# Agent attention with a soft mixture of experts: 32-column tensor products, an earlier normalisation, column maxima read from PSUM, and a new order of all steps

## The chip, the cores and the metric

One core of one Trainium2 chip runs the whole kernel; nothing is shared with other cores. The metric is the device time of one execution in microseconds (us): first to last instruction plus what the launch adds. One execution is also recorded by the hardware profiler, and the views below are of that one.

## The reference

Four batches of 11456 tokens with 128 channels go through attention by way of 49 agents, and the result `x` goes through a soft mixture of 8 experts with 4 slots each.

```python
def sm(a, b):                              # softmax of scaled scores
    s = scale * (a @ b.transpose(0, 2, 1))
    e = np.exp(s - s.max(-1, keepdims=True))
    return e / (e.sum(-1, keepdims=True) + 1e-09)
agent_v = sm(agents, k) @ v                # (4, 49, 128)
x = sm(q, agents) @ agent_v                # reshaped to (45824, 128)
logits = x @ phi                           # 32 slots
d = softmax of logits over the tokens (columns)
c = softmax of logits over the slots (rows)
slot_out[e] = relu((d.T @ x)[e] @ w1[e]) @ w2[e]
return c @ slot_out                        # (45824, 128)
```

All data are 32-bit floats.

## The kernel before

The tokens of a batch lie in four streams and are cut into six groups, five of 16 cells and one of 10; a cell is 128 tokens. There are 24 such groups of keys and values (the k side) and 24 of queries (the q side). The work is written as small steps with two-letter names; the table `ORDER` (1280 steps before) is one fixed sequence of them, and each engine executes its share of that sequence strictly in order. Buffers with numbered slots (`BUFS`) are handed out along the same sequence. All large loads go through the queue of SyncE (SP), also in that sequence.

**The k side of a group.** `kx` and `kv` load the tiles `kt` and `vt` (1 MB each). `ks` makes scores `sk` on TensorE (PE) in 32-column tiles, four of which lie side by side in the array. `km` takes their maximum on VectorE (DVE, `kmx`); `kt`, `kr`, `kb`, `kn` bring the running maximum of each agent through a transpose (`mt`), a row (`row`) and a broadcast (`mc`). `ke` is the exponential on ScalarE (ACT, `es`), `kT` its transpose on DVE (`et`; for group 0 on PE and ACT, steps `kP`), `kE` the product with the values (`ev`), `kA` the accumulation. After a batch `kg` and `kh` make agent_v and its product with phi, kept as `bd_m`.

**The q side.** `qx` loads `qt`, `qs` makes scores `sq`, `qt` transposes them on DVE into `pt`, `qm` takes the maximum over the agents. The exponential is done either on ACT cell by cell with its sum (`qE`, the groups in `DEN_ACT`) or by GpSimd (POOL) and ACT over the whole tile (`qu`, `qe`), with the sum on DVE (`qw`). `qp` transposes `pt` on PE into `tp`, `qc` copies it out, `ql` multiplies by `bd_m` into `lq`. For the 19 groups in `SWAP` `qn` transposes `lq` on DVE into `lt`, in two halves, and `qg` multiplies `lt` by the reciprocal sums `rt` on POOL; the last five groups use another form of `ql` and `qn` (tile `lp`). `lt` then holds the logits. `qM` takes the maximum of every slot (`cm`), `cr` that of every token; `cu` and `ce` write exp(logit − row maximum) into `x_all`.

**Rounds.** One or two q groups make a round, 13 in all. `r1` merges the column maxima, `r2`, `r3` reduce them over the tokens, `rx`, `r4`, `r5` broadcast them back, `ru` and `re` make the column weights `dt`, `rm` multiplies them by `rt`, and `rg` adds their product with `pt` to `gp`.

**The end.** After the last round the rounds are put on one scale, the experts run (`w1`, `w2`, steps m…), and 24 chunks of output leave: sums and reciprocals `cd`, scaling on POOL, transposes `ct`, the product `po`, copies `ot`, and a store.

Of the kernel before, what the change touches and what calls it, by code (L numbers as in the profile page):

```python
# [16 lines left out]
S = E * SE  # L17
# [17 lines left out]
CO_AB = CO_ID + P  # L35
# [121 lines left out]
def tile_agent_attn_soft_moe(ctx, tc, qT, kT, vL, agT, phi, w1, w2, cst, out):  # L157
# [7 lines left out]
    nc.scalar.dma_start(out=ag, in_=agT)  # L165
    nc.scalar.dma_start(out=cs, in_=cst)
# [9 lines left out]
    sel_r = [cs[0:2, CO_R + 3 * i:CO_R + 3 * i + 3] for i in range(2)]  # L176
# [5 lines left out]
    m_all = keep.tile([S, NR + 1], F32, name="m_all")  # L182
    av = keep.tile([A, B, C], F32, name="av")
    bd_m = [keep.tile([P, 2, S + 1], F32, name=f"bd_m{i}") for i in range(2)]
    si = keep.tile([P, E, 32], F32, name="si")
    v_.memset(si, 0.0)
    for t in bd_m:
        v_.tensor_copy(out=t[:, :, S], in_=mask_ab)
# [17 lines left out]
    def op(fam, i, eng, cost, fn, deps=(), takes=(), gives=()):  # L206

        k = (fam,) + tuple(i)
        ops[k] = {"eng": eng, "cost": cost, "deps": list(dict.fromkeys(deps)), "takes": takes,
                  "gives": gives, "reads": {}}  # L210
        for tag, first in gives:
            ops[first]["reads"][tag] = ops[first]["reads"].get(tag, 0) + 1
        fns[k] = fn
        return k
# [20 lines left out]
    den_act = [i for i in DEN_ACT if i in SWAP]  # L235
# [3 lines left out]
    def k_ops(i):  # L239
# [25 lines left out]
        def kt():  # L265
            k["mt"] = tile_("m", [2, P], f"mt_{i}")
            t_.transpose(k["mt"], k["mx"], ident)

        def kr():
            k["row"] = sm.tile([2, 32], F32, name=f"row_{i}", tag="row")  # L270
            v_.tensor_reduce(out=k["row"], in_=k["mt"].rearrange("p (q a) -> p a q", q=4),
                             axis=AX.X, op=ALU.max)
            if g:
                v_.tensor_tensor(out=k["row"], in0=k["row"], in1=prev["row"], op=ALU.max)  # L274
# [28 lines left out]
        def kP(h):  # L303
            k["tp", h] = tile_("a", [P, 4, P], f"ktp_{i}_{h}")
            for j in range(4):
                t_.transpose(k["tp", h][:, j, :], k["e"][:, h, P * j:P * j + P], ident)
# [803 lines left out]
```

## Time and profile before

| | |
|---|---|
| runs | 332.74, 334.86, 336.35 us (median 334.86) |
| profiled execution, span | 332.0 us; the page gives no other time for it, so the median of the runs lies 2.9 us above its span |
| busy in the span | PE 274.5, DVE 264.7, ACT 195.7, POOL 139.8 us |
| moved | 104.18 MB, 314 GB/s over the span |
| granted TensorE clock | mean 0.934 |

Engines run beside each other, so busy times don't add up to the span; an engine that is busy in a stage for nearly all of it can set that stage's length. A group line of the profile names the source line, the engine, the operation, the tile written and the tiles read, then `xcount | busy us, mean ns of one | idle before it and what ended that idle time`. A 32-bit matmul of the source appears as two MATMUL instructions. PEld is the loading of weights, which lies beside PE. A matmul's form, such as 128\*32, gives the rows and columns of the array that it uses.

### The profile page before, as it was taken

The numbers are of one execution on the slowest core, as the hardware profiler recorded it, in microseconds if no ns is written. First come the engines' busy times: TensorE is split into PE (matmuls) and PEld (weight loads), VectorE is DVE, ScalarE is ACT, GpSimd is POOL, SyncE is SP. The second block draws the span as 40 slices with busy tenths as digits, with TensorE's granted clock in tenths as the row PEclk, the third lists the DMA queues.
The fourth block names the chain that finished last, engine by engine and source line by source line (L and its number), as shares of the span: only waits on it lengthen the run. The fifth ranks groups of instructions, "written<-read, shape, count | busy, mean of one in ns | idle before, by whom it ended". The sixth has DMA issues, their size and how long they took to land.

```text
span 332.0 us, 9455 instructions
## 1 busy us (share of the span) xinstructions
PE 274.5 (83%) x3821; PEld 152.7 (46%) x3821; DVE 264.7 (80%) x580; ACT 195.7 (59%) x613; POOL 139.8 (42%) x158
## 2 busy tenths in 40 slices
PE   1978978988998989898999989998978885866740
PEld 0234455544554455365556447467765551121210
DVE  0754675989998898999998988999949649998830
ACT  2496333484979685686956986374442246655540
POOL 0100001418382454638236938566886205343400
PEclk9999999999999999999999999999968999678555
DMA  7999899999979649989839990699400019999996
GB/s 298 423 409 359 319 395 418 421 410 402 393 275 397 216 135 423 411 340 358 360 121 424 360 400 5 218 408 424 176 0 2 2 77 415 423 414 422 410 424 265
DMA packets 15451, 104.18 MB, mean 314 GB/s; under 512 B 1840, under 2 KB 1968, under 8 KB 4016
## 3 DMA queue, kind: packets, MB, share of 16 engines
q1 hardware_dynamic: 14976, 102.95, 77.3%
q8 instruction: 30, 0.49, 0.6%
q10 hardware_dynamic: 432, 0.63, 0.5%
q14 instruction: 13, 0.11, 0.1%
HBM read 79.98 MB, written 23.59 MB: 312 GB/s over the span
## 4 chain that ended last, share of the span: by engine, by line
DVE 44%; PE 29%; DMA 11%; ACT 7%; POOL 4%; issue 3%; SPq 0%; ACTq 0%; DVEq 0%; POOLq 0%
PE ev L318 5%; DVE cm L536 5%; DMA out<-ot 5%; DVE pt L434 5%; PE sk L230 5%; PE sq L230 4%; ACT pt L460 3%; DVE mx L439 3%; DVE kmx L262 3%; DVE et L300 3%; DVE rm L541 3%; PE po L1025 3%; DMA qt<-qT 3%; DMA cs<-cst 3%; DVE row L274 3%
## 5 line engine op out<-in xcount | busy, mean ns | idle before, releaser
L460 ACT ACTIVATE pt<-pt,mx 128x49 f32<-128x49 f32 x160 | 51.4, 328 | 10.6 <-DVE mx L439 10.5
L230 PE MATMUL sq<-qt,ag 128*32 128x512 f32 (+1 forms) x384 | 48.1, 600 | 8.0 <-ACT ag L168 6.7
L1025 PE MATMUL po<-ct,sob 32*128 32x512 f32 (+1 forms) x192 | 35.4, 819 | 17.9 <-DVE ct L888 13.0
L230 PE MATMUL sk<-kt,ag 128*32 128x512 f32 (+1 forms) x384 | 46.9, 573 | 1.5 <-issue 0.9
L318 PE MATMUL ev<-vt,et 128*64 128x129 f32 x720 | 45.1, 276 | 3.3 <-DVE lt L490 1.4
L1030 ACT COPY ot<-po 128x1536 f32<-128x1536 f32 (+1 forms) x24 | 32.6, 1359 | 24.5 <-DVE ot L1029 24.5
L318 PEld LDWEIGHTS ev<-vt,et 128*64 128x64 f32 x720 | 39.3, 136 | 10.6 <-issue 2.3
L444 POOL TENSOR_TENSOR pt<-pt,mx 128x784 f32<-128x784 f32 (+1 forms) x14 | 19.3, 1378 | 57.6 <-DVE mx L439 55.6
L882 POOL TENSOR_TENSOR x_all<-x_all,cd 128x512 f32<-128x512 f32 (+1 forms) x24 | 23.9, 994 | 41.6 <-DVE cd L877 38.7
L262 DVE TENSOR_REDUCE kmx<-sk 128x1 f32<-128x512 f32 (+1 forms) x48 | 30.7, 641 | 9.2 <-PE sk L230 8.8
L544 POOL TENSOR_TENSOR x_all<-lt,rm 128x512 f32<-128x512 f32 (+1 forms) x24 | 24.2, 1015 | 25.3 <-DVE rm L541 21.4
L434 DVE STREAM_TRANSPOSE pt<-sq 128x512 f32<-128x512 f32 (+1 forms) x48 | 31.3, 660 | 4.1 <-PE sq L230 3.9
L511 ACT COPY pT<-tp 128x512 f32<-128x512 f32 (+1 forms) x48 | 25.4, 557 | 11.7 <-PE tp L504 11.5
L640 POOL TENSOR_TENSOR dt<-lt,mb 128x512 f32<-128x512 f32 (+1 forms) x24 | 28.7, 1212 | 7.4 <-ACT mb L634 7.1
L300 DVE STREAM_TRANSPOSE et<-es 128x512 f32<-128x512 f32 (+1 forms) x46 | 29.6, 650 | 1.9 <-ACT es L289 1.9
L460 ACT ACTIVATION_READ_ACCUMULATOR pt<-pt,mx 128x1 f32 x160 | 30.5, 191 | 0.0
L1025 PEld LDWEIGHTS po<-ct,sob 32*128 32x128 f32 x192 | 10.4, 240 | 42.5 <-ACT ot L1030 42.2
L289 ACT ACTIVATE es<-sk,nm 128x512 f32<-128x512 f32 (+1 forms) x48 | 29.3, 650 | 0.2
L495 POOL TENSOR_TENSOR lt<-lt,rt 128x512 f32<-128x512 f32 (+1 forms) x19 | 19.0, 999 | 23.0 <-DVE lt L490 22.9
L504 PE MATMUL tp<-cs,pt 128*128 128x128 f32 x180 | 27.2, 282 | 0.7 <-ACT pt L450 0.5
L504 PEld LDWEIGHTS tp<-cs,pt 128*128 128x128 f32 x180 | 19.3, 141 | 14.4 <-issue 4.2
L1029 DVE COPY ot<-po 128x512 f32<-128x512 f32 (+1 forms) x24 | 15.4, 643 | 12.6 <-DMA out<-ot 7.7
(123 smaller groups left out, 462.8 us busy)
## 6 DMA issues: line engine op xcount, KB each, us to landing
out<-ot SPq DMA_DIRECT2D x21, 1024.0 KB, 6.8
vt<-vL SPq DMA_DIRECT2D x20, 1032.0 KB, 10.0
qt<-qT SPq DMA_DIRECT2D x20, 1024.0 KB, 8.4
kt<-kT SPq DMA_DIRECT2D x20, 1024.0 KB, 7.0
w1s<-w SPq DMA_DIRECT2D x4, 1024.0 KB, 11.3
w2s<-w SPq DMA_DIRECT2D x4, 1024.0 KB, 12.0
vt<-vL SPq DMA_DIRECT2D x4, 645.0 KB, 8.4
kt<-kT SPq DMA_DIRECT2D x4, 640.0 KB, 7.5
```

The costliest lines, as they stand in the source:

```text
L230: t_.matmul(sp[32 * q4:32 * q4 + 32, :nt], ag[:, b, 32 * h:32 * h + 32], xv[:, q4, :], start=True, stop=True)
L262: v_.tensor_reduce(out=k["mx"][:, h:h + 1], in_=k["s"][h][:, :nt], axis=AX.X, op=ALU.max)
L289: s_.activation(out=k["e"][:, h, :nt], in_=k["s"][h][:, :nt], func=AF.Exp, bias=k["nm"][:, h:h + 1])
L300: v_.transpose(out=k["et"][:, :n, 32 * h:32 * h + 32], in_=k["e"][:, h, :nt].rearrange("p (t a) -> p t a", a=32))
L318: t_.matmul(k["ev"][o:o + 64, :], k["et"][:, c, :], k["v"][:, c, :], start=c < 2, stop=c >= n - 2)
L434: v_.transpose(out=q["pt"][:, :n, 32 * h:32 * h + 32], in_=q["s"][h][:, :nt].rearrange("p (t a) -> p t a", a=32))
L460: s_.activation(out=x, in_=x, func=AF.Exp, bias=q["mx"][:, c:c + 1], accum_out=q["dn"][:, c:c + 1])
L504: t_.transpose(q["tp", h][:, (c - h0) // 2, :], q["pt"][:, c:c + 2, :].rearrange("p c a -> p (c a)"), ident)
L511: s_.copy(out=q["pT"][:, h0 // 2:h1 // 2, :], in_=q["tp", h][:, :(h1 - h0) // 2, :])
L640: eng.tensor_tensor(out=q["dt"][:, :n], in0=q["lt"][:, :n, :], op=ALU.subtract, in1=r["mb"].unsqueeze(1).to_broadcast([P, n, S]))
L1025: t_.matmul(po[:, r, :32 * n], z["sob"][32 * r:32 * r + 32, :], z["ct", j][32 * r:32 * r + 32, :32 * n], start=True, stop=True)
L1030: s_.copy(out=ov[:, 1:4], in_=po[:, 1:4, :32 * n])
```

## The change

Four things are done at once, and with them the table `ORDER` (1248 steps now) is a new sequence throughout.

1. **32-column products.** `kE` is split into two 32-column matmuls per cell; the broadcasts `kb` and `r4` read zero-padded rows of 128 partitions in place of 2 or 32; the transpose path of group 0 (`KT_PE`) and the `lp` form of the last five groups are gone.
2. **Running row maximum.** The previous row goes through PE beside the new maxima, and one DVE reduction over five blocks replaces a reduction and a `tensor_tensor`.
3. **Normalised ahead of the transposes.** `qw` (ACT) and `qr` make the reciprocal, the new step `qN` multiplies `pt` on POOL, then `qp` follows. `qg` and `rm` are gone. `DEN_ACT` has 12 groups in place of 10.
4. **Column maxima from PSUM.** `qM` reduces `lq` as it lies in PSUM to one number per partition; `r1` and `rx` are gone, `r6` is new, and `qv` transposes both halves at once.

At the start the constants come in two pieces, `ag` goes through SP, and two copies into `bd_m` are gone.

```diff
-                o = 64 * (c % 2)
-                t_.matmul(k["ev"][o:o + 64, :], k["et"][:, c, :], k["v"][:, c, :], start=c < 2,
-                          stop=c >= n - 2)
+                for h in range(2):
+                    o = 64 * (c % 2) + 32 * h
+                    t_.matmul(k["ev"][o:o + 32, :], k["et"][:, c, 32 * h:32 * h + 32],
+                              k["v"][:, c, :], start=c < 2, stop=c >= n - 2)
...
+            if g:
+                t_.matmul(k["mt"][:, P:nq], ident[:, 0:2], prev["row"], start=True, stop=True)
+            t_.matmul(k["mt"][:, 0:P], k["mx"], ident, start=True, stop=True)
...
-            if g:
-                v_.tensor_tensor(out=k["row"], in0=k["row"], in1=prev["row"], op=ALU.max)
...
+        def qN():
+            x = q["pt"][:, :n, 0:A]
+            nc.gpsimd.tensor_tensor(out=x, in0=x, op=ALU.mult,
+                                    in1=q["rt"][:, :n].unsqueeze(2).to_broadcast([P, n, A]))
+            nc.gpsimd.memset(q["pt"][:, :n, A:A1], 1.0)
...
-            v_.tensor_reduce(out=q["cm"], in_=q["lt"][:, :n, :].rearrange("p c s -> p s c"),
-                             axis=AX.X, op=ALU.max)
+            v_.tensor_reduce(out=rs[ri]["cm"][:, g - gs[0]:g - gs[0] + 1], axis=AX.X, op=ALU.max,
+                             in_=q["lp"][:, :n // 2].rearrange("p j e t -> p (j e t)"))
...
+        e = o("qw", (), "A", qw, deps=(e,))
+        e = o("qr", (), "V", qr, deps=(e,))
+        e = o("qN", (), "G", qN, deps=(e,))
+        p0 = o("qp", (0,), "P", lambda: qp(0), deps=(e,), takes=("a",))
```

Two lines of the new table, from its start: `kx ks.0 ks.1 kx km.0 qx@1 km.1 qx kt kr ks.0 kb kn ke.0 qs.0@1 …`; the old one began `qx qx qs.0 qs.1 qx qt.0 qs.0 qt.1 qm kx …`.

On PE, in the second batch, these instructions stood in a row before (`ev` is the product with the values, `mt` and `mc` the running maximum, `tp` a transpose of `pt`, `t` the two steps of a round's maximum):

```order
L230 MATMUL sq_1_1140<-qt_1_1057,ag 32x512 x4
L267 MATMUL mt_1158<-cs,kmx_1105 2x128
L318 MATMUL ev_1160<-vt_1008,et_1091 64x129 x16
L279 MATMUL mc_1192<-cs,row_1178 32x3 x4
L504 MATMUL tp_0_1198<-cs,pt_1015 128x128 x4
L504 MATMUL tp_1_1206<-cs,pt_1015 128x128 x4
L619 MATMUL t_1_1217<-cs,cmr_0_1145 32x128
L230 MATMUL sk_0_1219<-kt_5_1154,ag 32x320 x4
L230 MATMUL sk_1_1227<-kt_5_1154,ag 32x320 x4
L481 MATMUL lq_0_1240<-pT_1138,bd_m_69 32x4x32 x8
L630 MATMUL t_1_1255<-cs,mrep_1250 128x32
```

About the same place of the program reads so now:

```order
L225 MATMUL sk_1_1303<-kt_5_967,ag 32x320 x4
L475 MATMUL lq_1308<-pT_1288,bd_m_75 32x4x32 x8
L475 MATMUL lq_1308<-pT_1288,bd_m_75 32x32 x8
L275 MATMUL mc_1336<-cs,row_70 32x3 x4
L304 MATMUL ev_1353<-vt_1209,et_1161 32x129 x32
L264 MATMUL mt_1386<-row_70,cs 2x32
L265 MATMUL mt_1386<-cs,kmx_1330 2x128
L225 MATMUL sq_0_1392<-qt_2_1176,ag 32x512 x4
L275 MATMUL mc_1399<-cs,row_71 32x3 x4
L225 MATMUL sk_0_1412<-kt_0_1254,ag 32x512 x4
L547 MATMUL t_2_1421<-cs,cm_1251 1x128 x2
```

Before, the output width goes 32, 2, 64, 32, 128, 32, 128; now the whole stretch has outputs of at most 32 columns, and `ev` counts 32 matmuls in place of 16.

On DVE, in the third batch before (`lt` are logits, `cm` and `cmr` column maxima of a group and of a round, `row` the running maximum):

```order
L490 STREAM_TRANSPOSE lt_2026<-lq_1_1878 128x256
L434 STREAM_TRANSPOSE pt_2032<-sq_1_2034 128x16x32
L271 TENSOR_REDUCE row_2060<-mt_2040 2x32
L274 TENSOR_TENSOR row_2060<-row_2060,row_1901 2x32
L536 TENSOR_REDUCE cm_2065<-lt_2026 128x32
L439 TENSOR_REDUCE mx_2075<-pt_2032 128x16
L261 MEMSET sk_0_2043 64x32
L262 TENSOR_REDUCE kmx_2105<-sk_0_2043 128x1
L614 TENSOR_TENSOR cmr_0_2129<-cm_1949,cm_2065 128x32
```

And now, around the corresponding round:

```order
L482 STREAM_TRANSPOSE lt_2039<-lq_2001 128x512
L490 TENSOR_REDUCE cm_2054<-lq_2001 128x1
L409 STREAM_TRANSPOSE pt_1921<-sq_1_2048 128x16x32
L409 STREAM_TRANSPOSE pt_2072<-sq_0_2027 128x16x32
L448 RECIPROCAL rt_2011<-rt_2011 128x10
L414 TENSOR_REDUCE mx_2120<-pt_1921 128x16
L296 STREAM_TRANSPOSE et_2122<-es_2118 128x16x32
L490 TENSOR_REDUCE cm_2054<-lq_2096 128x1
L482 STREAM_TRANSPOSE lt_2137<-lq_2096 128x512
L257 TENSOR_REDUCE kmx_2139<-sk_0_2113 128x1
L551 TENSOR_REDUCE row_72<-t_4_2141 1x32
```

The column maximum reads `lq` in PSUM and may stand on either side of the transpose; the merges (`cmr`, the second `row`) are gone.

On POOL, in the second batch before (`dn` are sums, `mx` the agents' maxima):

```order
L495 TENSOR_TENSOR lt_976<-lt_976,rt_1019 128x512
L444 TENSOR_TENSOR pt_1156<-pt_1156,mx_1189 128x16x49
L446 MEMSET pt_1156 128x16
L464 TENSOR_SCALAR pt_1015<-dn_1100 128x16
L640 TENSOR_TENSOR dt_1267<-lt_804,mb_1264 128x512
```

There `rt` multiplies `lt`, and POOL also finishes sums. Now, in the second batch too:

```order
L572 TENSOR_TENSOR dt_1747<-lt_1262,mb_1521 128x512
L498 TENSOR_TENSOR x_all<-lt_858,rm_1573 128x512
L452 TENSOR_TENSOR pt_1433<-pt_1433,rt_1530 128x16x49
L454 MEMSET pt_1433 128x16
L419 TENSOR_TENSOR pt_1785<-pt_1785,mx_1806 128x16x49
```

The multiplication by `rt` has moved from `lt`, behind the transposes, to `pt`, ahead of them.

More of the change, by code (lines that the diff above doesn't have):

```diff
@@ L34 @@
 CO_ID = 0
-CO_AB = CO_ID + P
+CO_MK = CO_ID + P
+CO_R = CO_MK + 2
+CO_AB = CO_R + 6
 CO_ST = CO_AB + P
@@ L111 @@
-KT_PE = (0,)
-SWAP = tuple(range(19))
-DEN_ACT = tuple(range(0, 19, 2))
+    "kt": 2, "vt": 3, "qt": 3, "es": 1, "et": 2, "pt": 8, "pT": 3, "lt": 5, "dt": 2,
+    "ct": 4, "s": 4, "a": 3, "m": 1, "hs": 2, "ht": 3,
+}
+DEN_ACT = tuple(range(0, 24, 2))
 FILL = (0, 4, 4, 3, 4, 3, 7)
@@ L164, in tile_agent_attn_soft_moe @@
     ph = keep.tile([P, S], F32, name="ph")
-    nc.scalar.dma_start(out=ag, in_=agT)
-    nc.scalar.dma_start(out=cs, in_=cst)
+    nc.sync.dma_start(out=ag, in_=agT)
+    nc.scalar.dma_start(out=cs[:, :CO_AB], in_=cst[:, :CO_AB])
+    nc.scalar.dma_start(out=cs[:, CO_AB:], in_=cst[:, CO_AB:])
     nc.scalar.dma_start(out=ph, in_=phi)
@@ L175, in tile_agent_attn_soft_moe @@
     mask_ab = cs[:, CO_MK:CO_MK + 2]
-    sel_r = [cs[0:2, CO_R + 3 * i:CO_R + 3 * i + 3] for i in range(2)]
+    sel_r = [cs[:, CO_R + 3 * i:CO_R + 3 * i + 3] for i in range(2)]
     sel_ts = cs[0:S, CO_TS:CO_TS + P]
@@ L181, in tile_agent_attn_soft_moe @@
     g_all = keep.tile([P, NR, A1], F32, name="g_all")
-    m_all = keep.tile([S, NR + 1], F32, name="m_all")
+    m_all = keep.tile([P, NR + 1], F32, name="m_all")
+    rows = [keep.tile([P, 32], F32, name=f"row{i}") for i in range(5)]
     av = keep.tile([A, B, C], F32, name="av")
-    bd_m = [keep.tile([P, 2, S + 1], F32, name=f"bd_m{i}") for i in range(2)]
+    bd_m = [keep.tile([P, 2, S], F32, name=f"bd_m{i}") for i in range(2)]
     si = keep.tile([P, E, 32], F32, name="si")
     v_.memset(si, 0.0)
-    for t in bd_m:
-        v_.tensor_copy(out=t[:, :, S], in_=mask_ab)
+    v_.memset(m_all, 0.0)
+    for t in rows:
+        v_.memset(t, 0.0)
     ps = ExitStack()
@@ L204, in tile_agent_attn_soft_moe, with op @@
     slots, now = {}, [None]
-    def op(fam, i, eng, cost, fn, deps=(), takes=(), gives=()):
+    def op(fam, i, eng, fn, deps=(), takes=(), gives=()):
         k = (fam,) + tuple(i)
[L209 to L212, printed above, removed]
+        ops[k] = {"eng": eng, "deps": list(dict.fromkeys(deps)), "takes": takes, "gives": gives}
         fns[k] = fn
@@ L301, in kT_ @@
                          in_=k["e"][:, h, :nt].rearrange("p (t a) -> p t a", a=32))
[L303 to L306, printed above, removed]
-        def kQ(h):
-            if h == 0:
-                k["et"] = tile_("et", [P, QC, 64], f"et_{i}")
-            s_.copy(out=k["et"][:, :, 32 * h:32 * h + 32].rearrange("p (j q) a -> p j q a", q=4),
-                    in_=k["tp", h].rearrange("p j (q a) -> p j q a", q=4))
         def kE():
@@ L472, in qr @@
-        def qr():
-            q["rt"] = rp.tile([P, QC], F32, name=f"rt_{i}", tag="rt", bufs=BUFS["lt"] + 2)
-            v_.reciprocal(out=q["rt"][:, :n], in_=q["pt"][:, :n, A])
-        def qL(h):
-            h0, h1 = half(h)
-            lp = q["lp", h] = tile_("a", [P, 4, 2, 32], f"lq_{i}_{h}")
-            for e in range(2):
-                for q4 in range(4):
-                    t_.matmul(lp[32 * q4:32 * q4 + 32, :(h1 - h0) // 2, e, :],
-                              bd_m[b % 2][:, e, 0:S],
-                              q["pT"][:, h0 // 2:h1 // 2, 32 * q4:32 * q4 + 32],
-                              start=True, stop=True)
@@ L486, in qv @@
[L486 to L498 removed]
+                              accum_out=q["rt"][:, c:c + 1])
@@ L605, in r_ops @@
+        l1 = o("ql", (1,), "P", lambda: ql(1), deps=(c1, mm, l0), gives=(("pT", c0),))
+        before = [("qM", i - 1)] if g != gs[0] else []
+        f = o("qM", (), "V", qM, deps=[l1] + before, gives=(("a", l0),))
+        v = o("qv", (), "V", qv, deps=(f,) if last else (l1,), takes=("lt",),
+              gives=(("a", l0),))
+        f = o("cr", (), "V", cr, deps=(v,))
+        f = o("cu", (), "G", cu, deps=(f,), gives=(("lt", v),))
+        o("ce", (), "A", ce, deps=(f,))
     def r_ops(ri):
@@ L608, in r_ops, with r6 @@
         i = grp[-1]["i"]
-        def r1():
-            r["cmr"] = grp[0]["cm"]
-            for j, q in enumerate(grp[1:]):
-                cmr = sm.tile([P, S], F32, name=f"cmr_{ri}_{j}", tag="cmr", bufs=2)
-                v_.tensor_tensor(out=cmr, in0=r["cmr"], in1=q["cm"], op=ALU.max)
-                r["cmr"] = cmr
         def r2():
-            r["t1"] = tile_("m", [S, P], f"t1_{ri}")
-            t_.transpose(r["t1"], r["cmr"], ident)
+            r["t1"] = tile_("m", [1, 2, P], f"t1_{ri}")
+            for j in range(len(grp)):
+                t_.matmul(r["t1"][:, j, :], r["cm"][:, j:j + 1], ident, start=True, stop=True)
         def r3():
-            v_.tensor_reduce(out=m_all[:, ri:ri + 1], in_=r["t1"], axis=AX.X, op=ALU.max)
-        def rx():
-            r["mrep"] = sm.tile([S, P], F32, name=f"mrep_{ri}", tag="mrep", bufs=2)
-            s_.copy(out=r["mrep"], in_=m_all[:, ri:ri + 1].to_broadcast([S, P]))
+            r["row"] = rows[3 + ri % 2]
+            v_.tensor_reduce(out=r["row"][0:1, :], axis=AX.X, op=ALU.max,
+                             in_=r["t1"][:, :len(grp)].rearrange("p j (q s) -> p s (j q)", s=S))
         def r4():
-            r["t2"] = tile_("m", [P, S], f"t2_{ri}")
-            t_.matmul(r["t2"], r["mrep"], ident[0:S, 0:S], start=True, stop=True)
+            r["t2"] = tile_("m", [P, S + 1], f"t2_{ri}")
+            e0 = sel_r[0][:, 0:1]
+            for q4 in range(4):
+                t_.matmul(r["t2"][32 * q4:32 * q4 + 32, 0:S], e0.to_broadcast([P, 32]),
+                          r["row"], start=True, stop=True)
+            t_.matmul(r["t2"][0:S, S:S + 1], r["row"], e0, start=True, stop=True)
         def r5():
             r["mb"] = sm.tile([P, S], F32, name=f"mb_{ri}", tag="mb", bufs=2)
-            s_.copy(out=r["mb"], in_=r["t2"])
+            s_.copy(out=r["mb"], in_=r["t2"][:, 0:S])
+        def r6():
+            s_.copy(out=m_all[0:S, ri:ri + 1], in_=r["t2"][0:S, S:S + 1])
         def ru(q):
@@ L739, in z_wt @@
         lo, hi = (0, n0) if e else (n0, NR + 1)
-        s_.activation(out=wt[:, lo:hi], in_=m_all[:, lo:hi], func=AF.Exp, bias=nm[:, e:e + 1])
+        s_.activation(out=wt[:, lo:hi], in_=m_all[0:S, lo:hi], func=AF.Exp, bias=nm[:, e:e + 1])
     def z_wr(e):
@@ L896, in tile_agent_attn_soft_moe, with o @@
     steps = [0]
-    def o(name, eng, cost, fn, **kw):
+    def o(name, eng, fn, **kw):
         steps[0] += 1
-        return op(name, (steps[0],), eng, cost, fn, **kw)
+        return op(name, (steps[0],), eng, fn, **kw)
     ends = [(f, i) + x for i in range(NT - 3, NT) for f, x in (
         ("ks", (1,)), ("ke", (1,)), ("kT", (1,)), ("kE", ()))]
-    wx = [o("w1", "D", 2910, lambda x=x: z_w1(x), deps=ends) for x in range(4)]
-    wy = [o("w2", "D", 2910, lambda x=x: z_w2(x), takes=("qt",) if x < 3 else (),
+    wx = [o("w1", "D", lambda x=x: z_w1(x), deps=ends) for x in range(4)]
@@ L930, in tile_agent_attn_soft_moe @@
-    g2 = f
-    f = o("l1", "P", 140, z_l1, deps=(f, gl))
-    f = o("l2", "V", 100, z_l2, deps=(f,), gives=(("s", gl),))
-    f = sp = o("l3", "P", 220, z_l3, deps=(f, ("kh", NT - 1, 4)), takes=("s",))
-    si_ = o("l4", "V", 100, z_l4, deps=(f, ff), gives=(("s", sp),))
-    d0 = o("d0", "V", 280, z_d0, deps=(g2, de))
+    ms = o("ms", "G", z_ms, deps=ends)
+    f = nme = o("en", "V", lambda: z_nm(1), deps=[("r6", ri) for ri in range(n0)])
+    f = o("en", "A", lambda: z_wt(1), deps=(f,))
+    f = wr = o("en", "P", lambda: z_wr(1), deps=(f,), takes=("m",))
@@ new lines, in tile_agent_attn_soft_moe @@
+    f = o("en", "V", lambda: z_ws(1), deps=(f,), gives=(("m", wr),))
+    f = ge = o("en", "V", lambda: gscale(0, n0), deps=[f] + [("rc", x) for x in range(n0)])
+    f = f2 = o("en", "P", z_gt, deps=(f,), takes=("s",))
+    f = o("en", "A", z_gc, deps=(f,), gives=(("s", f2),))
+    f = f2 = o("en", "P", z_si, deps=[f] + [("kh", NG * x + NG - 1, 4) for x in range(B - 1)],
+               takes=("s",))
+    sc = o("en", "A", z_sc, deps=(f,), gives=(("s", f2),))
+    de = o("en", "V", z_de, deps=(ge,))
@@ new lines, in tile_agent_attn_soft_moe @@
+    f = o("nm", "V", lambda: z_nm(0), deps=[nme] + [("r6", ri) for ri in range(n0, NR)])
+    w_ = o("wt", "A", lambda: z_wt(0), deps=(f,))
+    f = wr = o("wr", "P", lambda: z_wr(0), deps=(w_,), takes=("m",))
+    ws = o("ws", "V", lambda: z_ws(0), deps=(f,), gives=(("m", wr),))
+    f = o("f0", "V", z_f0, deps=(w_,))
+    f = f1 = o("f1", "P", z_f1, deps=(f, sc), takes=("m",))
+    ff = o("f2", "V", z_f2, deps=(f,), gives=(("m", f1),))
+    f = o("gl", "V", lambda: gscale(n0, n1), deps=[ws] + [("rc", x) for x in range(n0, n1)])
```

441 lines of the change are left out of this document (173 added, 268 removed).

## The prediction

> **What bounds the kernel now.** I read the windows first, because the page's shares average over stages with different limits. The columns are the stretch, then the busy time of PE, weight loads, DVE, ACT and POOL, the granted clock, the share of the DMA engines, and GB/s.
>
> ```profile
> 10.00:80.00 70.00, 61.77 (x802) 33.24 (x796) 51.88 (x109) 40.35 (x154) 12.10 (x16) 1.00 0.99 395
> 80.00:215.00 135.00, 126.17 (x2123) 71.88 (x2119) 126.16 (x265) 98.74 (x381) 75.84 (x87) 1.00 0.78 303
> 215.00:250.00 35.00, 31.12 (x428) 25.09 (x425) 29.84 (x78) 17.91 (x45) 27.55 (x30) 0.91 0.60 248
> 250.00:268.00 18.00, 15.81 (x267) 10.66 (x266) 13.15 (x32) 4.36 (x9) 6.12 (x6) 0.98 0.01 3
> 268.00:332.00 64.00, 36.42 (x201) 11.10 (x199) 43.40 (x98) 32.62 (x24) 18.00 (x18) 0.71 0.89 369
> ```
>
> Up to 80 us the DMA engines are full (0.99) and PE waits 8.2 us in 70. From 80 to 215 PE and DVE are both busy for 126 of 135 us: two engines at 93%, so relief of one alone would soon run into the other. From 250 to 268 the experts run; from 268 on the output is stored. Then the chain that ended last, from the page:
>
> ```profile
> DVE 44%; PE 29%; DMA 11%; ACT 7%; POOL 4%; issue 3%; SPq 0%; ACTq 0%; DVEq 0%; POOLq 0%
> ```
>
> DVE and PE make up 73% of it, which is the same answer. Last the waits, for the start:
>
> ```profile
> DVE bd_m L188 <- DMA cs<-cst: 8.8, 1, 8.8
> PE sq L230 <- ACT ag L168: 6.7, 1, 6.7
> ```
>
> PE starts at 6.7 us, DVE's real work only when the constants have landed.
>
> **The sum** goes by PE: its busy time from 10 to 268 us, with what the change adds and removes, plus its idle time. Then I ask whether another engine would come out longer. Before, PE is busy for 61.8 + 126.2 + 31.1 + 15.8 = 234.9 of these 258 us and idle for 23.1.
>
> *PE's products.*
>
> ```profile
> L318 PE MATMUL ev<-vt,et 128*64 128x129 f32 x720 | 45.1, 276 | 3.3 <-DVE lt L490 1.4 <-ACT pT L511 0.7 <-DVE et L300 0.6
> L481 PE MATMUL lq<-pT,bd_m 128*32 128x128 f32 (+1 forms) x608 | 20.6, 269 | 0.0
> L660 PE MATMUL gp<-pt,dt 128*32 128x50 f32 x720 | 12.3, 213 | 2.0 <-POOL dt L651 1.4 <-DVE acc L324 0.4 <-DVE dt L651 0.2
> L517 PE MATMUL lp<-bd_m,pT 128*128 128x66 f32 x74 | 8.9, 276 | 0.0
> L306 PE MATMUL ktp<-cs,es 128*128 128x128 f32 x8 | 1.3, 287 | 0.9 <-ACT et L311 0.6 <-ACT es L289 0.2
> L481 PEld LDWEIGHTS lq<-pT,bd_m 128*32 128x32 f32 x608 | 15.4, 110 | 6.7 <-issue 4.7 <-ACT bd_m L360 0.3 <-DVE m_all L622 0.2
> ```
>
> `ev` goes from 720 instructions in 64 columns (45.1/720 = 62.6 ns each) to 1440 in 32 columns. No row has exactly that shape; `lq` has the same array form and 128 elements in place of 129, at 20.6/608 = 33.9 ns. So `ev` becomes 1440 × 33.9 = 48.8 us: **+3.7**. The ends are `gp`'s 17.1 ns (−20.5 us; it streams only 50) and no gain per instruction (62.6 ns, +45). I take `lq`, the nearest by far, which also loads new weights for every product.
>
> From `gp` to `lq`, 16.8 ns for 78 more elements make 0.215 ns per element, and 6 ns that stay when the stream is short. [...]
>
> The `lp` form goes (−8.9); its five groups need 80 more products of `lq`, 160 instructions at 33.9 ns (+5.4). In the rounds 24 transposes of one column stand in place of 13: 11 more at about 0.27 us, the mean of `lq` and `lp` alike, are **+3**, between 0 and +8, as five broadcasts also stand in place of one per round and 20 extra rows of 32 columns beside `mt`. The transposes of group 0 on PE go (−1.3). Products together: 3.7 − 8.9 + 5.4 + 3 − 1.3 = **+1.9**.
>
> *PE's changes of form.* From the timeline of PE, start and duration:
>
> ```profile
> 164.71 1.06 PE L230 MATMUL sk<-kt,ag 128*32 128x512 f32 x8
> 165.59 1.04 PE L230 MATMUL sq<-qt,ag 128*32 128x512 f32 x8
> 171.26 1.06 PE L230 MATMUL sk<-kt,ag 128*32 128x512 f32 x8
> 172.26 0.66 PE L504 MATMUL tp<-cs,pt 128*128 128x128 f32 x4
> 172.85 1.99 PE L318 MATMUL ev<-vt,et 128*64 128x129 f32 x32
> ```
>
> Eight score instructions take 0.88 us from start to start when the next has the same form, and 1.00 when a 128-column transpose follows: 0.12 us for the change. Counted along PE's lists up to the first output product, the form changes 196 times before and 75 times now, because `ev`, `mc` and the rounds' steps no longer leave the 32-column form. 121 × 0.12 = **−14.5 us**. The ends are 0 (the time is inherent in the small steps, or the new weights hold `ev` back) and 0.15 us, −18.2: the four transposes stream 4 × 128 elements, half of the 8 × 512 / 4 that the scores stream side by side in 0.88 us, and take 0.59 in place of 0.44.
>
> So PE needs 234.9 + 1.9 − 14.5 = 222.3 us.
>
> *PE's idle time* was 8.2 us while DMA was full, 8.8 from 80 to 215 and 6.1 after. Whether it stays depends on DVE:
>
> ```profile
> L536 DVE TENSOR_REDUCE cm<-lt 128x32 f32<-128x512 f32 (+1 forms) x24 | 23.5, 980 | 0.4 <-POOL lt L498 0.2 <-POOL lt L495 0.2
> L490 DVE STREAM_TRANSPOSE lt<-lq 128x256 f32<-128x256 f32 (+1 forms) x38 | 14.7, 395 | 0.0
> L274 DVE TENSOR_TENSOR row<-row,row 2x32 f32<-2x32 f32 x20 | 10.3, 516 | 0.7
> L469 DVE TENSOR_REDUCE pt<-pt 128x16 f32<-128x784 f32 (+1 forms) x9 | 7.6, 844 | 1.0 <-PE mt L267 1.0
> L529 DVE TENSOR_TENSOR lt<-lp,rt 128x256 f32<-128x256 f32 (+1 forms) x10 | 4.0, 405 | 0.2
> L474 DVE RECIPROCAL rt<-pt 128x16 f32<-128x16 f32 (+1 forms) x19 | 3.9, 213 | 0.9 <-POOL pt L464 0.9
> L614 DVE TENSOR_TENSOR cmr<-cm,cm 128x32 f32<-128x32 f32 x11 | 3.7, 339 | 0.0
> L470 DVE TENSOR_SCALAR pt<-pt 128x16 f32<-128x16 f32 (+1 forms) x9 | 3.7, 407 | 0.3
> L651 DVE TENSOR_TENSOR dt<-dt,rt 128x512 f32<-128x512 f32 (+1 forms) x2 | 2.6, 1363 | 0.0
> L527 DVE RECIPROCAL rt<-lp 128x8 f32<-128x8 f32 (+1 forms) x10 | 1.9, 192 | 0.0
> L528 DVE COPY pt<-lp 128x8 f32<-128x8 f32 (+1 forms) x10 | 1.2, 120 | 0.0
> L262 DVE TENSOR_REDUCE kmx<-sk 128x1 f32<-128x512 f32 (+1 forms) x48 | 30.7, 641 | 9.2 <-PE sk L230 8.8
> L434 DVE STREAM_TRANSPOSE pt<-sq 128x512 f32<-128x512 f32 (+1 forms) x48 | 31.3, 660 | 4.1 <-PE sq L230 3.9
> ```
>
> The first eleven rows go: 77.1 us. In come 24 maxima over PSUM of the shape of `kmx` (24 × 0.641 = 15.4), 24 whole transposes like `pt` (15.8), 12 sums (10.1 at 844 ns) and 24 reciprocals (5.1), two more transposes of `et` (1.3), and about 2, an allowance, for wider reductions. 77.1 − 49.7 = **27 us less on DVE**: from 221.0 to 194 in this stretch. That engine is then at 80% and no longer ties with PE. I let PE's idle time from 80 to 215 fall from 8.8 to 5 and keep the rest: 19.3 us. The ends are 12 (every wait but the DMA's halves) and 23.
>
> The stretch is thus 222.3 + 19.3 = **241.6 us in place of 258, −16.4**.
>
> *Would another engine be longer?*
>
> ```profile
> L460 ACT ACTIVATE pt<-pt,mx 128x49 f32<-128x49 f32 x160 | 51.4, 328 | 10.6 <-DVE mx L439 10.5
> L284 ACT ACTIVATE nm<-mc 128x3 f32<-128x3 f32 x24 | 4.1, 172 | 24.6 <-PE mc L279 24.6
> L626 ACT COPY mrep<-m_all 32x128 f32<-32x128 f32 x13 | 3.7, 288 | 8.8 <-DVE m_all L622 8.8
> L450 ACT ACTIVATE pt<-pt 128x784 f32<-128x784 f32 (+1 forms) x14 | 11.2, 800 | 5.9 <-POOL pt L444 5.9
> L444 POOL TENSOR_TENSOR pt<-pt,mx 128x784 f32<-128x784 f32 (+1 forms) x14 | 19.3, 1378 | 57.6 <-DVE mx L439 55.6
> L495 POOL TENSOR_TENSOR lt<-lt,rt 128x512 f32<-128x512 f32 (+1 forms) x19 | 19.0, 999 | 23.0 <-DVE lt L490 22.9
> L651 POOL TENSOR_TENSOR dt<-dt,rt 128x512 f32<-128x512 f32 (+1 forms) x22 | 22.4, 1026 | 1.4 <-ACT dt L645 1.4
> HBM read 79.98 MB, written 23.59 MB: 312 GB/s over the span
> ```
>
> ACT: 32 more cells of `qE` at 51.4/160 = 0.32 us (+10.3), 24 `qw` and 13 `r6` at about 0.172 (+6.4), two `qe` at 0.80 and all of `L626` less (−5.3): 161 us become 173, 72% of the stretch. POOL: 24 `qN` of the shape of `L444` (+33.1) for 19.0 + 22.4 and two `L444` less (−2.8): about 11 us less. DMA: 80 MB at the 395 GB/s of the first window are 203 us. None reaches 241; PE stays the bound.
>
> *The ends of the program.* The DVE copies that wait for the constants go, and `ag` leads SP's queue; but PE, not DVE, starts first, and DMA is full afterwards. I count −1 us, between 0 and −3. The output stage runs the same instructions, and is held by its stores at 0.89 of the DMA engines: 0, at most +2 if the first scalings on POOL, which now stand after the last `cu`, come late.
>
> Sum: 332.0 − 16.4 − 1 = 314.6 us of span; with the 2.9 us by which the median lies above the span, 317.5: **318 us**.
>
> **Rivals.**
>
> - *The changes of form cost nothing that can be saved.* For it: many of the 0.12 us stand beside instructions so short that PE would wait anyway. Then PE needs 236.8 us, and with 20 us idle the stretch is 257: 333 us, no change.
> - *Every instruction of the split `ev` has a fixed cost on PE.* Its new weights would lie on PE's path and not beside it: the weight loads of `lq` take 15.4/608 = 25 ns each, 18 us for 720 more, in place of the 3.7 that I count: 332 us. Against it: `lq` has such a load for every product and keeps to 33.9 ns. [...]
> - *More goes than I count.* 0.15 us for each change and 12 us idle: 234.9 + 1.9 − 18.2 + 12 = 230.6 us, 27.4 less; 306.5 us. For it: DVE lets go in the stage where both were full.
> - *ACT binds in the last batches.* The table brings q groups forward there, 12 of 24 with the cell-by-cell exponential at 5.1 us a group. If ACT holds PE back for 8 us over that stage: 326 us.
> - *Slower: `qN` stands in front of PE's queue.* PE executes in order, and `tp` now waits for `qw`, `qr` and a multiplication of about 1.4 us on POOL, where it waited only for the exponential; behind a waiting `tp` stand the scores and `ev` that DVE needs. Each of 24 groups would have to hold PE for 0.7 us to eat up the 17 us; at 1.7 us the time is 318 + 41 − 17 = 342. Against it: eight `pt` slots allow the table to put `qp` well after `qN`, and POOL is at 56% in the middle stage.
>
> **How the numbers follow.** The forecast gets 0.60 (its own range 308 to 326), the case without savings at the changes of form 0.07, the fixed cost 0.04, the larger gain 0.14, ACT 0.08, the slower case 0.07. The range from 305 to 331 leaves out the slower case, most of the two cases near 333 and some of the larger gain; the far ends of `ev`, some −20 and +45 us, lie outside it, since only shapes unlike it give them. One per cent, 3.3 us, is about what a measurement of this kernel can tell from no change. Faster by more than that: 0.83; same: 0.10, from the two cases near 333 us; slower: 0.07.
>
> **What would show it.** Right: `ev` near 34 ns per instruction with 1440 of them; score groups at 0.88 us from start to start beside `ev`; DVE's `cm` near 640 ns and its busy time near 238 us in the span; PE at 93% or more in the middle stage with DVE near 80%; the output stage as long as before. Wrong: an `ev` at 40 ns or more, PE waits that end with POOL's `pt`, or an ACT over 90% in the fourth batch.

## The result, and the profile after

The changed kernel takes **319.24 us** (median of 4 runs, 317.43 to 322.14) against 334.66 us (332.74 to 336.35) before: a ratio of 0.953, 95% interval 0.946 to 0.960. The prediction was 318 us. Its profiled execution has a span of 320.0 us and took 322.14 us, the upper end of its runs. (Ratios here and below leave disturbed runs out, medians do not.)

The windows, columns as before:

```profile
10.00:80.00 70.00, 62.99 (x1166) 37.33 (x1162) 53.58 (x104) 42.29 (x171) 15.45 (x16) 1.00 1.00 404
80.00:215.00 135.00, 126.51 (x2903) 88.66 (x2895) 119.11 (x246) 109.52 (x461) 74.38 (x79) 1.00 0.83 329
215.00:235.00 20.00, 12.98 (x284) 10.66 (x283) 8.89 (x22) 6.79 (x21) 11.31 (x12) 0.82 0.59 244
235.00:250.00 15.00, 14.46 (x156) 8.19 (x155) 7.88 (x23) 6.42 (x17) 4.07 (x5) 0.67 0.01 2
250.00:256.00 6.00, 6.00 (x127) 5.77 (x126) 4.17 (x13) 1.55 (x4) 3.27 (x4) 1.00 0.01 4
256.00:320.00 64.00, 38.57 (x199) 10.85 (x197) 45.53 (x101) 32.60 (x24) 18.82 (x19) 0.68 0.89 369
```

The output stage starts at 256 us in place of 268. PE is busy for 63.0 + 126.5 + 13.0 + 14.5 + 6.0 = 222.9 us of the 246 before it, 12.0 less than before, and idle for 23.1, as much as before. A new stretch looks bad: from 215 to 235 PE does 13.0 us of work in 20, and behind it the granted clock is 0.67. The chain, and the waits of PE (waits in the output stage and some short ones left out):

```profile
PE 64%; DMA 12%; DVE 9%; issue 6%; ACT 5%; POOL 1%; DVEq 0%; SPq 0%
```

```profile
PE sk L225 <- DMA kt<-kT: 8.6, 2, 7.6
PE gp L585 <- issue: 6.3, 5, 3.4
PE ev L304 <- issue: 5.4, 4, 2.1
...
PE lq L475 <- issue: 1.6, 1, 1.6
PE ev L304 <- DMA vt<-vL: 1.5, 2, 1.0
PE mt L265 <- DVE kmx L257: 1.3, 2, 0.8
```

DVE has all but left the chain (44% to 9%), and most waits for it are gone. In their place stands **"issue"**, in which PE waits for nothing that the profile names: 14.4 of the 23.1 us that PE is idle ahead of the output, where it was 0.9 of 23.1:

```profile
PE sk L230 <- issue: 0.9, 1, 0.9
```

That was no part of the prediction. The groups that it sized:

```profile
L304 PE MATMUL ev<-vt,et 128*32 128x129 f32 x1440 | 45.9, 274 | 7.2 <-issue 5.4 <-DMA vt<-vL 1.5 <-ACT pT L467 0.2
L475 PE MATMUL lq<-pT,bd_m 128*32 128x128 f32 (+1 forms) x768 | 27.5, 268 | 1.6 <-issue 1.6
L585 PE MATMUL gp<-pt,dt 128*32 128x50 f32 x720 | 16.0, 221 | 6.5 <-issue 6.3
L490 DVE TENSOR_REDUCE cm<-lq 128x1 f32<-128x512 f32 (+1 forms) x24 | 15.3, 640 | 1.5 <-PE mc L275 0.6 <-PE lq L475 0.5 <-PE t L560 0.3
```

### The profile page after: what moved, and what is told of

Read it like the earlier page. It is cut to its first block, busy times and chain, and to the rows that moved or that the text cites. A ratio compares the mean times of both kernels' runs of the same rounds, so it can differ in the third digit from the quotient of the medians.

```text
span 320.0 us, 11457 instructions
## 1 busy us (share of the span) xinstructions
PE 263.9 (82%) x4822; PEld 162.1 (51%) x4822; DVE 240.1 (75%) x511; ACT 200.9 (63%) x697; POOL 127.5 (40%) x136
## 4 chain that ended last, share of the span: by engine, by line
PE 64%; DMA 12%; DVE 9%; issue 6%; ACT 5%; POOL 1%; DVEq 0%; SPq 0%
PE sk L225 12%; PE sq L225 12%; PE ev L304 11%; DMA out<-ot 7%; PE tp L460 7%; PE lq L475 6%; DMA kt<-kT 4%; PE gp L585 3%; DVE ot L948 2%; DVE ct L808 2%; ACT ot L949 2%; PE hp L748 2%; PE po L944 2%; ACT pt L437 2%; DVE cd L795 2%
## 5 line engine op out<-in xcount | busy, mean ns | idle before, releaser
L437 ACT ACTIVATE pt<-pt,mx 128x49 f32<-128x49 f32 x192 | 61.7, 329 | 1.3 <-DVE mx L414 1.3
L225 PE MATMUL sk<-kt,ag 128*32 128x512 f32 (+1 forms) x384 | 53.3, 600 | 9.8 <-DMA kt<-kT 8.6
L452 POOL TENSOR_TENSOR pt<-pt,rt 128x784 f32<-128x784 f32 (+1 forms) x24 | 34.5, 1440 | 60.4 <-DVE rt L448 52.5
L304 PE MATMUL ev<-vt,et 128*32 128x129 f32 x1440 | 45.9, 274 | 7.2 <-issue 5.4
L944 PE MATMUL po<-ct,sob 32*128 32x512 f32 (+1 forms) x192 | 37.8, 871 | 14.3 <-DVE ct L808 9.3
L304 PEld LDWEIGHTS ev<-vt,et 128*32 128x32 f32 x1440 | 40.5, 109 | 13.6 <-issue 8.3
L437 ACT ACTIVATION_READ_ACCUMULATOR pt<-pt,mx 128x1 f32 x192 | 36.9, 192 | 0.0
L419 POOL TENSOR_TENSOR pt<-pt,mx 128x784 f32<-128x784 f32 (+1 forms) x12 | 16.2, 1354 | 39.1 <-DVE mx L414 39.1
L475 PE MATMUL lq<-pT,bd_m 128*32 128x128 f32 (+1 forms) x768 | 27.5, 268 | 1.6 <-issue 1.6
L475 PEld LDWEIGHTS lq<-pT,bd_m 128*32 128x32 f32 x768 | 22.4, 110 | 7.5 <-issue 4.7
## 6 DMA issues: line engine op xcount, KB each, us to landing
vt<-vL SPq DMA_DIRECT2D x20, 1032.0 KB, 10.2
```

Source lines behind the costliest of these rows:

```text
L225: t_.matmul(sp[32 * q4:32 * q4 + 32, :nt], ag[:, b, 32 * h:32 * h + 32], xv[:, q4, :], start=True, stop=True)
L304: t_.matmul(k["ev"][o:o + 32, :], k["et"][:, c, 32 * h:32 * h + 32], k["v"][:, c, :], start=c < 2, stop=c >= n - 2)
L437: s_.activation(out=x, in_=x, func=AF.Exp, bias=q["mx"][:, c:c + 1], accum_out=q["rt"][:, c:c + 1])
L452: nc.gpsimd.tensor_tensor(out=x, in0=x, op=ALU.mult, in1=q["rt"][:, :n].unsqueeze(2).to_broadcast([P, n, A]))
L475: t_.matmul(q["lp"][32 * q4:32 * q4 + 32, h0 // 2:h1 // 2, e, :], bd_m[b % 2][:, e, :], q["pT"][:, h0 // 2:h1 // 2, 32 * q4:32 * q4 + 32], ...
L944: t_.matmul(po[:, r, :32 * n], z["sob"][32 * r:32 * r + 32, :], z["ct", j][32 * r:32 * r + 32, :32 * n], start=True, stop=True)
```

## What "issue" is

The page's DMA queues, first of the kernel before, then of the changed one (packets, MB, share):

```profile
q8 instruction: 30, 0.49, 0.6%
```

```profile
q8 instruction: 38, 0.62, 0.8%
```

All 38 packets are of 16,384 bytes. PE runs 4822 products with as many weight loads, and 9644 / 38 = 254 instructions for each packet: this queue brings PE its program, 127 products at a time. Put in order of time, the stalls put down to "issue" come behind the 1107th, 1361st, 1488th, 1868th, 2122nd ... product, each a multiple of 127 after the last, to within two. The longest, on PE's timeline:

```profile
224.14 0.34 PE L585 MATMUL gp<-pt,dt 128*32 128x50 f32 x10
227.92 0.56 PE L585 MATMUL gp<-pt,dt 128*32 128x50 f32 x16 [3.44 <-issue]
```

And the DMA queues from 220.8 to 225.4 us, then from 225.4 to 228:

```profile
q1 hardware_dynamic: 267, 1.94, 101.5%
```

```profile
q1 hardware_dynamic: 78, 0.50, 47.7%
q8 instruction: 1, 0.02, 2.6%
```

In the first stretch only data moves, w1 and w2, with the DMA engines full; in the second comes one packet of instructions, which starts at 225.5 and takes 1.1 us. PE goes on 1.3 us after it. At all twelve stalls PE starts again 1.3 to 1.5 us (once 1.6) after such a packet has landed, and the packet starts 2.6 to 5.1 us after PE began the block before. The starts of the other blocks, counted off between the stalls, show the same: where the DMA engines were under 10% busy in the 2 us before it, a packet starts 0.4 to 1.2 us after the block before began, and where they were at 99% or more ahead of the output stage, 2.6 to 5.1 us. So one block ahead is asked for, its packet queues with the data, and a block of `ev`, 127 × 31.9 ns = 4.1 us, is over too early. Before the change PE waited 0.9 us for its instructions ahead of the output, after it 14.4.

## Experiments

Theory A is this supply of instructions; the rivals are the prediction's own terms. "Idle" below means PE, from 10 us to the first output product. The kernel before took 333.5 us beside experiments 1 to 4, 335.1 on another chip beside 5 to 8, and 334.8 beside the last; the ratios take this out.

**1. `ev` 64 columns wide again**, in the changed kernel:

```diff
-                for h in range(2):
-                    o = 64 * (c % 2) + 32 * h
-                    t_.matmul(k["ev"][o:o + 32, :], k["et"][:, c, 32 * h:32 * h + 32],
-                              k["v"][:, c, :], start=c < 2, stop=c >= n - 2)
+                o = 64 * (c % 2)
+                t_.matmul(k["ev"][o:o + 64, :], k["et"][:, c, :], k["v"][:, c, :], start=c < 2,
+                          stop=c >= n - 2)
```

> The changed kernel with the products of ev 64 columns wide again, as before the change: 720 products fewer, that is 1440 instructions of PE and five to six packets of 16 KB on PE's instruction queue fewer (38 to about 32). Theory A (PE waits for its own instructions): the idle time put down to 'issue' falls from 14.5 us before the output stage to 1 to 4, the form of the tile changes 134 times instead of 73 (61 x 0.12 = +7.3 us), ev itself costs about 0.8 us less, and the clock in the tail is granted longer: 311 to 318 us. Theory B (the prediction's sum, in which instruction supply costs nothing): +7.3 for the changes of form, -3.7 for the width of ev, 323 us.

311.9 us (310.9 to 312.9), ratio 0.937 (0.931 to 0.943); 32 packets.

```profile
L303 PE MATMUL ev<-vt,et 128*64 128x129 f32 x720 | 44.3, 275 | 0.6 <-DMA vt<-vL 0.4 <-ACT pT L466 0.2
```

"Issue" falls to 4.9 us, a little less far than expected, PE is busy for 225.6 us in place of 223.7, and the kernel is 7 us faster (5 by the ratios). Theory A holds; the split of `ev`, a part of the change, costs time.

**2. `lq` once for both halves**, in the changed kernel (the first half emits nothing):

```diff
-            h0, h1 = half(h)
+            h0, h1 = 0, n
             if h == 0:
                 q["lp"] = tile_("a", [P, QC // 2, 2, 32], f"lq_{i}")
+                return
```

> The changed kernel with the 16 products of lq for a group made as 8, over both halves at once with 256 columns moving instead of 128, at the place of the second half: 384 products fewer, three packets of instructions fewer. Theory A (instruction supply): idle 'issue' time falls by 2 to 5 us, 314 to 318 us. Theory B (PE is bound by what it streams, and the number of instructions doesn't matter): 319 us, or 320 to 322 where the first half was made early enough to help DVE.

311.1 us (309.1 to 314.9), ratio 0.932 (0.923 to 0.942); the queue has 34 packets and "issue" is 6.8 us, 7.6 less than in the changed kernel, where 2 to 5 less was expected. `lq` itself also takes less, 24.8 us against 27.5:

```profile
L476 PE MATMUL lq<-pT,bd_m 128*32 128x256 f32 (+1 forms) x384 | 24.8, 369 | 0.0
```

But PE's busy time ahead of the output doesn't fall with it (225.0 us for 223.7): what is gained in the profiled execution is idle time, 15.2 us for 23.2.

**3. Narrow rows**, in the changed kernel, to price a change of form:

```diff
-                t_.matmul(k["mc"][32 * r:32 * r + 32, :], k["row"], sel_r[r % 2], start=True,
+                t_.matmul(k["mc"][32 * r:32 * r + 32, :], k["row"][0:2], sel_r[r % 2][0:2], start=True,
...
-                t_.matmul(r["t2"][32 * q4:32 * q4 + 32, 0:S], e0.to_broadcast([P, 32]),
-                          r["row"], start=True, stop=True)
-            t_.matmul(r["t2"][0:S, S:S + 1], r["row"], e0, start=True, stop=True)
+                t_.matmul(r["t2"][32 * q4:32 * q4 + 32, 0:S], e0[0:1].to_broadcast([1, 32]),
+                          r["row"][0:1], start=True, stop=True)
+            t_.matmul(r["t2"][0:S, S:S + 1], r["row"][0:1], e0[0:1], start=True, stop=True)
```

> The changed kernel with mc, and both products of a round's second step, contracted over two rows and one row again instead of over all 128 partitions: no instruction more or less, but the form of the tile changes 206 times before the output stage instead of 73. Theory C (a change of form costs 0.12 us of PE, as the prediction has it): +133 x 0.12 = 16 us of PE's busy time; some of it falls into waits for instructions that then end earlier, so 329 to 335 us. Rival (a change costs nothing that counts): 319 us, with PE's busy time as before.

323.2 us (318.3 to 325.0), ratio 0.963 (0.948 to 0.978): by time not told apart from the changed kernel. My count of 206 was wrong: the run's own trace has 138 changes (rows and columns of a form rounded up to 32, 64 or 128), 65 more. PE's busy time ahead of the output is 229.9 us, 6.2 more, with the clock at half for as long as in the changed kernel (17.1 us): **0.095 us** for a change, where the prediction took 0.12. Experiment 1 gives nearly the same: its trace has 112 changes, 39 more than the changed kernel's 73 and not the 61 more of the expectation; PE is busy for 2.0 us more and `ev` for 1.6 less, 0.09 us for a change.

**4. The split of `ev` alone**, in the kernel before (the lines of experiment 1, the other way round):

> The kernel before with one edit, ev split into products of 32 columns. Theory A: five to six packets of instructions more (30 to 36), idle 'issue' time up from 0.9 us to 3 to 8; theory C: 32 changes of form fewer, -3.8 us. Together 332 to 338 us; the prediction's terms alone (-3.8 for the form, +3.7 for the width) give 335, no change. It tells above all by its 'issue' time whether the split by itself brings the waits for instructions, or only the new order does.

338.9 us (335.9 to 339.7), ratio 1.019 (1.011 to 1.026): slower, just above the expected range. 36 packets, 4.8 us of "issue"; PE's busy time is 234.5 us, 1.3 less than before. So the split brings these waits in the old order too, and fewer changes of form do not pay for it.

**5. Both edits**, 1 and 2:

> The changed kernel with ev 64 columns wide and lq made once for both halves together: 1104 products fewer, 29 to 30 packets on PE's instruction queue. Theory A: the idle 'issue' time of PE before the output stage, 14.5 us in the changed kernel, 4.9 and 7.0 with one edit each, falls to 1 to 4 us, and the time to 303 to 309 us. Rival (past the first 8 us another engine or the end of the program sets the time, so the two do not add up): 310 to 312 us.

307.7 us (306.0 to 308.3), ratio 0.921 (0.914 to 0.929); 29 packets, 2.0 us of "issue". By the medians the edits add up to 11.5 of the 15.5 us that they gave singly, by the ratios to 3.1 of 3.6% of the time before.

**6. `w2` held back**, on top of 5; in the order w1 stands first and w2 behind the last round's row maxima (`r3`):

```diff
+        v_.memset(w2s[x][:, 0, 0, 0:1], 0.0)
         nc.sync.dma_start(out=w2s[x], in_=w2[x])
```

> As the kernel with both edits (ev 64 wide, lq once), and the transfers of the expert weights put in another order: w1 first, and the four of w2 (4 MB) held back until the last round's row maxima by a small write of DVE into their buffers. Theory A2 (PE's packets of instructions queue behind data in the DMA rings: in the changed kernel the packet asked for at 220.6 us starts at 225.5, while 8 MB of weights are under way): the idle 'issue' time of about 2.8 us among the last gp products falls under 1 us, the granted clock no longer drops to half right behind it, and the time is 3 to 8 us under that of the kernel with both edits alone. Rival 1 (the packet takes as long in quiet rings): no change within 1 us. Rival 2 (w2 now comes too late for the second layer): 2 to 6 us slower, with PE waiting for w2s.

303.8 us (302.5 to 306.8), ratio 0.913 (0.903 to 0.924), with no "issue" stall above 0.2 us at all; the interval overlaps with that of 5, so the time alone doesn't settle it. The packets are as many as in 5: what makes them late is the data in the queues. The two that stood behind the weights start 1.7 and 0.5 us after the block before began, in place of 4.3 and 4.6. (The other stall of 5, 0.8 us at 163 us, is gone too, but it came more than 30 us ahead of the weights and is not this edit's doing.) From the 2700th product, ahead of the weights, to the first output product the profiled execution takes 50.5 us, in 5 it was 52.5; the other 3.7 us by which its output starts earlier lie in front, where the edit changes nothing.

But the clock falls to half all the same, at 214.9 us for 10.2 us. PE stands still there from 214.1 us on, in a wait that isn't one for instructions:

```profile
PE wr L663 <- ACT wt L658: 2.4, 1, 2.4
```

So of theory A2 the queueing is shown, and the clock is not explained by it alone.

**7. The last `cr` later**, on top of 5. ACT's `wt` waits for DVE's `nmx` (step `nm`), and in DVE's list the last `cr` (`rm`) stands ahead of that. In the changed kernel DVE is idle in front of this `cr` from 225.2 us on, until POOL lets go a buffer:

```profile
233.71 0.49 DVE L495 TENSOR_REDUCE rm<-lt 128x10 f32<-128x320 f32 x1 [8.49 <-POOL x_all L498]
234.11 0.14 DVE L652 TENSOR_REDUCE nmx<-m_all 32x1 f32<-32x5 f32 x1
```

```diff
-r6 r5 cr rg.0 ru.0 nm
+r6 r5 rg.0 ru.0 nm
-l4 fl cu@22
+l4 cr fl cu@22
```

> As the kernel with both edits, and the last cr moved behind the merging of the rounds in DVE's list. In the changed kernel DVE stands 8.5 us at that cr (it waits for POOL's cu to let go a buffer), with nm behind it, for which ACT's wt and with it the last rg wait. Expected if this chain ends the reduction: 2 to 4 us under the kernel with both edits; if POOL's subtractions or PE's clock end it anyway: no change within 1 us.

301.9 us (301.7 to 303.5), ratio 0.906 (0.899 to 0.913): 6 us under kernel 5, more than expected; PE's wait for `wt` is gone, and the clock is at half for 6.8 us instead of 10.2. Two waits for instructions, 1.3 and 1.5 us, stay. In the profiled execution the stretch from the 2700th product to the output takes 50.5 us for 52.5, which is what was expected; 2.9 us more lie ahead of it, where the edit changes nothing. How much is due to the wait and how much to the clock isn't separated.

**8. More work for DVE**, in the changed kernel: the reduction in `cr` is made twice.

> The changed kernel with each cr made twice (the same values again): 24 more reductions, about 22 us more on DVE, 24 us being what the change took off it. Theory D (the relief of DVE is what lets PE run without waiting): PE waits for DVE again, 327 to 334 us. Rival (DVE has slack, and what holds PE is the supply of its instructions): 319 to 322 us, with the 'issue' time down where DVE's waits take its place.

324.6 us (318.7 to 327.6), ratio 0.962 (0.947 to 0.976): between the theories, and by time alone undecided. DVE's busy time is 254.3 us for 240.1, 14.2 more and not 22. PE's idle time up to the first output product rises from 23.2 to 27.4 us, with new waits for DVE (`row` 2.2, `lt` 1.8), while "issue" stays at 13.4. So in this profile 1 us of DVE is worth about 0.3 us of PE's waiting, and the waits for instructions do not hide behind DVE's.

**9. All of 5, 6 and 7**:

> As the kernel with both edits (ev 64 wide, lq once), with w2 held back and the last cr moved behind the merging as well. Each alone took the 307.7 us of that kernel to 303.8 and 301.9. Theory A2 (the two waits for instructions that are left in the tail, 1.3 and 1.5 us, come from packets behind the weights; the half clock follows a stretch in which PE stood still): both waits and the fall of the clock before the output stage go, 297 to 300 us. Rival (both edits cut the same wait): 301 to 303 us.

**299.5 us** (297.8 to 301.6, 6 runs), ratio 0.894 (0.889 to 0.899): faster than the kernel before and the changed one.

```profile
10.00:80.00 70.00, 66.14 (x851) 36.05 (x846) 55.94 (x108) 43.76 (x182) 16.51 (x18) 1.00 1.00 406
80.00:202.00 122.00, 121.14 (x2050) 77.34 (x2038) 112.44 (x233) 104.09 (x441) 69.07 (x73) 1.00 0.88 347
202.00:236.00 34.00, 31.66 (x639) 23.59 (x642) 25.87 (x69) 18.35 (x51) 23.58 (x24) 1.00 0.48 196
```

The output starts at 236 us, PE is at 99% in the middle, and the clock stays at 1.00 to the end of the tail. From the 2700th product to the output it takes 46.8 us, 5.7 less than in 5, where the two edits gave 2.0 each alone. One wait for instructions is left:

```profile
PE tp L456 <- issue: 1.7, 1, 1.7
```

Its packet starts 5.9 us after the block before began at 199.9, behind `w1`, whose loads are issued from 195.9 us on. So that part of the expectation held only for the clock.

## Why the prediction was right, step by step

- *Products of PE*: `ev` measured 31.9 ns each, 45.9 us (+0.8, where `lq`'s 33.9 ns had given +3.7); `lq` 27.5 (+6.9 with the added groups, predicted +5.4); `gp`, which I left alone, 12.3 to 16.0.
- *Changes of form*: the traces count 194 before and 73 after. At the 0.095 us of experiment 3 that is 11.5 us, not 14.5. PE's busy time came out at 222.9 us for 222.3 predicted; errors of one to four us in the terms cancel there.
- *PE's idle time*: **the step that failed.** I took 19.3 us, 3.8 less than before. All waits but "issue" fell from 22.2 to 8.7 us, far more than I allowed for DVE's relief; "issue", which had no term of its own, rose from 0.9 to 14.4. At experiment 8's 0.3 us the 24.6 us less of DVE are worth about 7 of the 13.5; that the rest comes from the new order is likely, but no run shows it. The stretch lost 12 us, not 16.4. That the median still came out near 318 is luck: it lies 0.8 us under the span of the profiled execution, the longest of the four, where I had put it 2.9 above.
- *The fixed cost per instruction of `ev`*, a rival at 0.04 priced at the 25 ns of a weight load: the row that I held against it, `lq` at 33.9 ns, shows a product that has arrived. The cost was in its arrival (7 us in experiment 1, in place of the 18), and `q8` with its 30 packets stood in the page that I read.
- *DVE*: 264.7 to 240.1 us in the span (predicted 238), `cm` at 640 ns as said. But it is busy for 88% of the middle stretch, not 80: the same work in less time. *ACT* rose by 5 us to 200.9, not 11; *POOL* fell by 12.3.
- *The ends*: the start is 0.9 us later, not 1 earlier (PE's first score waits 7.6 us for `kt`); the output stage is as long as before.
- *The slower case*, `qN` ahead of PE's queue: no wait of PE ends with POOL's `pt`, and `tp` waits 0.3 us in all. Its figure of 342 us was a slip of mine as well; 318 already holds the gain, so 318 + 41 is 359.
- *What would show it*: scores ahead of `ev` go on after 0.86 us (0.88 predicted), and PE is at 94% from 80 to 215 us:

```profile
176.35 1.04 PE L225 MATMUL sq<-qt,ag 128*32 128x512 f32 x8
177.21 1.95 PE L304 MATMUL ev<-vt,et 128*32 128x129 f32 x64
```

## What to carry to other kernels

Before an engine is given more and shorter instructions, divide its busy time by the packets on its instruction queue (7.9 us each before, 5.9 after): in the changed kernel a block of `ev` was worked off in 4.1 us, its packet started up to 5.1 us after the block before began and took about 1 us, and PE stalled, though each product took only 31.9 ns. When a sum comes out right, compare its terms: here errors of +14 and -10 us stood in one idle time. And where in-order engines merge at the end of a program, ask of each waiting instruction what stands behind it.

## What was not expected of the hardware

A packet of 16 KB took 0.9 to 1.4 us to move in the changed kernel, and in full DMA queues ahead of the output it took 2.6 to 5.1 us to begin; from the start of a block to the first instruction of the next that makes 5 to 7.5 us, so there 127 products of 32 ns, 4.1 us, were not kept supplied. And in the changed kernel a second cost came behind a stall: PE was idle for the 3.44 us up to 227.92, busy for 1% of the 3.4 us up to 227.85, and from there on the granted clock was 0.50 for 17.1 us, at the end of which 24 of the first layer's 32 products (L748) took 4.49 us; before the change all 32 took 3.8. Over a stretch as long as that stall ahead of the fall, PE had been busy for 87% in the kernel before (the fall at 243.9 us, to 0.50 for 6.8 us), for 76% in experiment 6 and for 56% in experiment 7, so a fall also came behind less idle time; in experiment 9 the 3.4 us up to 208.9, at 49%, had none behind them, with a granted clock of 1.00 from 202 to 236 us. Whether idle time brings the fall, and how much of it, no run shows.
